# First weights of the eight closing lists: plain transfers of SyncE with a register's address in place of indirect transfers of GpSimd

## The chip, the cores and the metric

One core of one Trainium2 chip runs the whole program. The metric is the device time of one execution in microseconds (us), lower is better. Engines: PE (matrix engine), ACT (ScalarE), DVE (VectorE), POOL (GpSimd), SP (SyncE, which here only issues transfers).

## The reference

The input is 8 sequences of 2496 rows of 256 values. The first half transforms each sequence by a Fourier transform along its rows, multiplies by a complex 256x256 matrix, shrinks small values to zero and transforms back. The second half is a mixture of eight experts whose tokens are chosen under a limit:

```python
cap = N // E                                   # 19968 // 8 = 2496
flat = (x @ w_gate).flatten()
for idx in np.argsort(-flat):                  # best logits first
    tok, e = int(idx) // E, int(idx) % E
    if assigned[tok] >= 0 or counts[e] >= cap: continue
    assigned[tok] = e; counts[e] += 1
for e in range(E):
    mask = assigned == e
    out[mask] = np.maximum(x[mask] @ w1[e], 0.0) @ w2[e]   # 256 -> 1024 -> 256
```

So which tokens an expert gets depends on the data, and so does, in this kernel, the order in which the experts are worked off.

## The kernel before

**Stages.** `phase_a` does the eight sequences (to about 550 us), writes the mixed rows to the DRAM tensor `YD` and the logits to `LG`. From the first four sequences `Router.early` takes 512 sure tokens for each expert; these eight "early lists" have a fixed expert number and their weights are loaded by plain transfers of SP (the branch `e is not None`, lines 638 to 640). After that come eight "closing lists" of 1984 tokens. `Router.closing(i, ...)` finds on DVE which expert fills up next and which tokens it gets; the expert's number is a value in the tile `wi` (lines 974 to 979: column 4 the number itself, columns 2 and 3 the row numbers of its first weights).

**Weights.** `Experts.load` (line 628) brings one expert's weights in four pieces of 512 KB: the first weights `w1` as m = 0 and 1 (k = 0), then the second weights `w2` as m = 0 and 1 (k = 1). Each goes into a tile `raw`, of which there are two (in the slots `xt`), so the `w2` pieces can come only when the `w1` pieces have been split. The split is an ACT cast (line 659) into a slot of `W`, and a DVE subtraction (line 660) of what the cast lost. `W` has eight slots (in `sp`, `sh`, `FG`), two experts' worth. In the closing lists the `w1` pieces are indirect transfers of POOL (line 651), row numbers from `wi`; the `w2` pieces are plain transfers of SP whose address comes from a register that SP loads from `wi` (lines 643 to 648). Ahead of every indirect transfer POOL runs `GAP` = 14 empty instructions.

**Tokens.** `Experts.run` (line 663) gathers a list's token rows by indirect transfers of POOL (line 673), 128 rows each. In closing lists two such gathers then go by SP to a DRAM tile `XG` (line 680) and come back in four transfers of 32 partitions each (line 684), so that DVE can transpose them by blocks (line 697); DVE and ACT split them (lines 698, 699). The first matmuls are line 726 (three per weight half: high x high, high x low, low x high), evicted by ACT and DVE (lines 730 to 733); the second matmuls are lines 745 to 748, evicted by ACT and DVE (lines 754, 755) and scattered to the output by indirect transfers of POOL (line 758).

**Order.** Nothing of the order is written by hand. `Plan.run` (line 142) is a list scheduler that runs when the program is built: every task has an engine, a duration, a priority `pos`, the buffers that it reads and writes, and for a transfer an entry for when its data land. It picks, again and again, the task that can start first, and so fixes each engine's queue. The entries here:

```python
LATE = dict(sp=1.71, raw=7.61, gather=2.51, scatter=6.24)
def moved(nbytes, run, lead=1.6, back=1.8, late=0.0, k=16): ...
def dma(...):  plan.add('SP', 0.4, ..., load=moved(nbytes, run, late=LATE['sp'] + late))
def ind(...):  plan.add('P', g + 1.05, ..., load=moved(nbytes, run, g + 1.2, 1.4, late))   # g = 0.71
```

An engine works off its queue strictly in that order; an instruction that waits holds up all behind it.

`general` at the end of the file is a second router that the program enters only if the first one found that it could not hold; it calls `load` without `block`.

Of the kernel before, what the change touches and what calls it, by code (L numbers as in the profile page):

```python
# [100 lines left out]
class Plan:  # L101
# [20 lines left out]
    def add(self, eng, dur, pos, emit, reads=(), writes=(), tail=0.0, after=(), uses=(), load=None, slack=0.0, port=False):  # L122
        t = Task()
        t.port = port
        t.eng, t.dur, t.pos, t.emit, t.tail = eng, dur, pos, emit, tail or self.DEPTH.get(eng, 0.0)
        t.load, t.slack = load, slack
        t.deps, t.writes, t.end = set(after), list(writes), None
        for b in reads:
            t.deps.update(b.writers)
        t.ords = set()  # L130
        for b in writes:
            if b.state:
                t.ords.update(b.users)
                b.users, b.writers = [], []
            b.writers.append(t)
        for b in list(reads) + list(writes) + list(uses):
            b.users.append(t)
        t.id = len(self.tasks)
        self.tasks.append(t)
        return t  # L140
# [141 lines left out]
LATE = dict(sp=1.71, raw=7.61, gather=2.51, scatter=6.24)  # L282
# [9 lines left out]
def moved(nbytes, run, lead=1.6, back=1.8, late=0.0, k=16): return lead, nbytes / run * (0.009 + 3.68e-5 * run if run <= 4096 else 7e-5 * run) / k, back + late  # L292
# [25 lines left out]
class Kit:  # L318
# [20 lines left out]
    def v(self, n, pos, emit, reads, writes, slack=0.0, port=True):  # L339
        return self.plan.add('V', 0.068 + n / 960, pos, emit, reads, writes, slack=slack, port=port and not any(b.psum for b in reads))  # L340
# [76 lines left out]
def load_logits(K, H, LG, LGb, b, pos):  # L417
    def load():
        for t, src in logit_parts(H.ML, LG, b): K.nc.sync.dma_start(t, src)  # L419
    K.plan.add('SP', 2.4, pos, load, [LGb[b]], [H.b_ML], load=moved(80e3, 100, late=LATE['sp']))  # L420
# [199 lines left out]
class Experts:  # L620
# [7 lines left out]
    def load(self, pos, e=None, wi=None, block=False):  # L628

        K, plan, v = self.K, self.K.plan, self.K.v  # L630
        W1, W2, reg = [], [], []
        for k in range(2):
            for m in range(2):
                r = K.sb("raw", [128, 1024])
                W = K.sb("W", *(([128, 2, 4, 256], F32R) if k else ([128, 2, 1024], F32R)))
                (W2 if k else W1).append(W)
                p = pos + (2 * k + m)
                if e is not None:
                    src = self.w[k][e].rearrange("(m p) f -> p m f", m=2)[:, m] if not k else self.w[k][e].rearrange("(g m p) d -> p g m d", g=2, m=4)[:, m]
                    K.dma(p, lambda r=r, src=src, k=k: K.nc.sync.dma_start(r.t.rearrange("p (m d) -> p m d", m=4) if k else r.t, src), 524e3, [], [r], run=1024 if k else 4096)  # L640
                elif k:

                    def ld(r=r, m=m, reg=reg):
                        if not m: reg.append(K.nc.values_load(wi.t[0:1, 4:5], engines=[mybir.EngineType.SP], min_val=0, max_val=7, skip_runtime_bounds_check_because="the number of an expert, held to at most 7 where it is written"))
                        K.nc.sync.dma_start(r.t.rearrange("p (m d) -> p m d", m=4), self.w[1][bass.ds(reg[0], 1)].rearrange("o (g m p) d -> p (o g) m d", g=2, m=4)[:, m])
                    q = K.dma(p, ld, 524e3, [wi], [r], run=1024)
                    if m: q.ords.add(last)
                    last = q
                else:
                    c = (2 if block else 0) + m  # L650
                    K.ind(p, lambda r=r, c=c: K.P.indirect_dma_start(out=r.t, out_offset=None, in_=self.rows, in_offset=bass.IndirectOffsetOnAxis(ap=wi.t[:, c:c + 1], axis=0)), 524e3, [wi], [r], run=4096, late=LATE['raw'])

                def part(i, o, k=k, r=r, W=W):
                    if k: return W.t[:, i - 1, 2 * o:2 * o + 2] if i else r.t.rearrange("p (m d) -> p m d", m=4)[:, 2 * o:2 * o + 2]

                    return (W.t[:, i - 1] if i else r.t)[:, 512 * o:512 * o + 512]
                for o in range(2):
                    h = plan.buf(None, None)
                    plan.add('A', .525, p + 1, lambda part=part, o=o: K.A.copy(part(1, o), part(0, o)), [r], [W, h], slack=SLACK['split'])
                    v(512, p + 1, lambda part=part, o=o: K.V.tensor_tensor(part(2, o), part(0, o), part(1, o), op=OP.subtract), [r, h], [W])  # L660
        return W1, W2
# [922 lines left out]
```

## Time and profile before

| | |
|---|---|
| median of 3 executions | 1431.98 us (1431.59 to 1433.9) |
| the profiled execution | 1429.78 us |
| its span in the trace | 1427.9 us |
| PE busy | 1410.4 us, 99% |
| DVE busy | 1086.0 us, 76% |
| ACT busy | 800.6 us, 56% |
| POOL busy | 454.6 us, 32% |

The profiled execution's own time is 1.9 us above its span. Busy time is only what an engine works; issuing transfers and waiting are not in it. The closing lists run from about 700 us to the end.

### The profile page before, as it was taken

How to read it: one execution, taken by the hardware profiler on the slowest of the kernel's cores; microseconds unless marked ns; L12 is line 12 of the kernel's file. 1: busy time of each engine (PE TensorE's matmuls, PEld its weight loads, DVE VectorE, ACT ScalarE, POOL GpSimd, SP SyncE). 2: the span in 40 equal slices, each digit the busy share in tenths (PEclk: the TensorE clock that was granted, in tenths of full speed). 3: DMA queues.
4: the chain of work that ended last, by engine and by line, in shares of the span. 5: the costliest groups of instructions: out<-in, count | busy, mean ns of one | idle time of the engine just before them, and what ended most of it. 6: DMA issues, size and time to landing. Idle time of an engine off the chain costs nothing.

```text
span 1427.9 us, 33182 instructions
## 1 busy us (share of the span) xinstructions
PE 1410.4 (99%) x9619; PEld 1192.4 (84%) x9619; DVE 1086.0 (76%) x3197; ACT 800.6 (56%) x1918; POOL 454.6 (32%) x430
## 2 busy tenths in 40 slices
PE   8999999999999999999999999999999999999997
PEld 7888888887888878888888888888888888888886
DVE  6888788776999977999999999988776463553442
ACT  5676878877788865446454544444436443343331
POOL 0012222222224345123535353544443425212112
PEclk9999999999999999999999999999999999999999
DMA  6787898787878685333636364545443353421000
GB/s 223 227 285 268 240 300 267 241 270 229 286 235 257 201 268 172 106 121 99 189 103 172 112 185 132 170 139 146 119 135 116 96 150 115 128 56 38 21 23 30
DMA packets 223778, 238.09 MB, mean 167 GB/s; under 512 B 95286, under 2 KB 187619, under 8 KB 223587
## 3 DMA queue, kind: packets, MB, share of 16 engines
q1 hardware_dynamic: 205793, 185.91, 42.7%
q0 software_dynamic: 17664, 49.86, 11.2%
q8 instruction: 78, 1.28, 0.4%
q14 instruction: 113, 0.93, 0.2%
q10 hardware_dynamic: 130, 0.11, 0.0%
HBM read 138.10 MB, written 97.71 MB: 165 GB/s over the span
## 4 chain that ended last, share of the span: by engine, by line
PE 90%; DVE 4%; DMA 2%; ACT 2%; issue 1%; SPq 1%; POOL 0%; POOLq 0%; DVEq 0%; ACTq 0%
PE b L726 27%; PE b L745 18%; PE b L746 9%; PE b L1231 7%; PE b L1260 4%; PE b L1215 4%; PE pt L726 4%; PE b L1239 3%; PE b L1297 3%; PE b L1174 3%; PE pt L745 2%; PE b L1320 1%; PE pt L746 1%; PE b L748 1%; SPq L419 1%
## 5 line engine op out<-in xcount | busy, mean ns | idle before, releaser
L1053 POOL TENSOR_TENSOR s2l<-s2c,s2h 120x512 fp32r<-120x512 f32 (+1 forms) x84 | 105.8, 1268 | 381.6 <-ACT s2h L1050 335.8
L758 POOL DMA_INDIRECT out_dram<-xTh,li x64 | 67.5, 1055 | 209.0 <-DVE xTh L755 112.1
L1231 PE MATMUL b<-wt,xTh 128*128 128x256 f32 x640 | 123.7, 290 | 0.4 <-DVE yT L1310 0.3
L1231 PEld LDWEIGHTS b<-wt,xTh 128*128 128x128 f32 x640 | 100.7, 190 | 9.6 <-issue 2.9
L1231 PE MATMUL b<-wt,xTl 128*128 128x256 f32 x320 | 92.1, 288 | 2.9 <-DVE xTl L1224 2.6
L758 POOL DMA_INDIRECT out_dram<-xTl,li x64 | 65.5, 1023 | 85.1 <-DVE xTl L755 44.1
L1215 PEld LDWEIGHTS b<-FG,sh 128*128 128x128 f32 x640 | 82.3, 191 | 10.4 <-issue 4.8
L1215 PE MATMUL b<-FG,sh 128*128 128x128 f32 x640 | 88.5, 277 | 1.2 <-DVE sh L1195 1.2
L754 ACT COPY xTh<-b 128x256 f32<-128x256 f32 x66 | 24.7, 374 | 104.4 <-PE b L746 94.7
L1260 PE MATMUL b<-y,FG 64*128 64x256 f32 x640 | 80.2, 389 | 0.0
L754 ACT COPY xTl<-b 128x256 f32<-128x256 f32 x69 | 25.8, 373 | 91.8 <-PE b L746 87.4
L1260 PEld LDWEIGHTS b<-y,FG 64*128 64x128 f32 x640 | 58.4, 186 | 14.5 <-issue 2.9
L1244 DVE TENSOR_TENSOR y<-b,sx 128x512 f32<-128x512 f32 x80 | 54.6, 684 | 17.8 <-ACT sx L1242 17.3
L755 DVE TENSOR_TENSOR xTl<-b,xTl 128x256 f32<-128x256 f32 x69 | 28.9, 418 | 51.6 <-ACT xTl L754 49.1
L1233 DVE TENSOR_TENSOR b<-b,bf 128x512 f32<-128x512 f32 x80 | 55.3, 691 | 16.6 <-PE b L1231 16.2
L1310 DVE STREAM_TRANSPOSE yT<-b 128x512 f32<-128x512 f32 x86 | 60.5, 707 | 9.2 <-ACT yst L1299 6.1
L1297 PE MATMUL b<-s2h,d 120*128 120x512 f32 (+1 forms) x168 | 66.6, 406 | 0.0
L1231 PEld LDWEIGHTS b<-wt,xTl 128*128 128x128 f32 x320 | 60.8, 190 | 5.4 <-DVE xTl L1224 5.0
L1239 PE MATMUL b<-wt,xTh 128*128 128x256 f32 x320 | 63.6, 291 | 0.4 <-DVE y L1244 0.4
L755 DVE TENSOR_TENSOR xTh<-b,xTh 128x256 f32<-128x256 f32 x66 | 27.6, 418 | 47.2 <-ACT xTh L754 47.2
L1299 ACT COPY yst<-b 117x512 f32<-117x512 f32 (+1 forms) x93 | 51.7, 563 | 16.3 <-DVE yT L1310 7.6
L1246 ACT ACTIVATE y<-y,ml 128x512 f32<-128x512 f32 x60 | 43.7, 729 | 20.3 <-DVE y L1244 19.7
(1148 smaller groups left out, 4985.4 us busy)
## 6 DMA issues: line engine op xcount, KB each, us to landing
xt<-in_moe_w_dram SPq DMA_DIRECT2D x48, 512.0 KB
T<-s4st SPq DMA_DIRECT2D x80, 256.0 KB
s2c<-T SPq DMA_DIRECT2D x80, 240.0 KB
YD<-yst SPq DMA_DIRECT2D x80, 234.0 KB
xt<-in_x_dram SPq DMA_DIRECT2D x35, 512.0 KB
sh<-T SPq DMA_DIRECT2D x35, 512.0 KB
T<-s1st SPq DMA_DIRECT2D x70, 240.0 KB
yT<-XG SPq DMA_DIRECT2D x64, 64.0 KB
```

What stands on the lines that cost most here:

```text
L726: T.matmul(ps.t[:, 0:w], lhsT=W1[m].t[:, a, 128 * ft:128 * ft + 128], rhs=x_.t[:, 0:w], start=q + m == 0, stop=q + m == 3)
L745: T.matmul(ps.t, lhsT=hh.t[:, u:u + 128], rhs=W2[ft // 4].t[:, :, ft % 4], start=ft == 0, stop=False)
L746: T.matmul(ps.t[:, 0], lhsT=hl.t[:, u:u + 128], rhs=w_[0], start=False, stop=ft == 7)
L755: v(256, pos + 1, lambda: V.tensor_tensor(o.t, ps.t[:, 0], o.t, op=OP.add), [ps, o], [o])
L758: ins = P.indirect_dma_start(out=self.out, out_offset=bass.IndirectOffsetOnAxis(ap=oi.t[0:M, oo + t:oo + t + 1], axis=0), in_=o.t[0:M], in ...
L1053: lambda: eng.tensor_tensor(lb[1](), src(), hb[1](), op=OP.subtract), [srcb, hb[0]], [lb[0]], port=True)
L1215: T.matmul(ps.t[:, :, dt, i], lhsT=sh[k // 8].t[:, k % 8, 128 * dt:128 * dt + 128], rhs=at(Ft, k), start=True, stop=True)
L1231: T.matmul(pc.t[:, c], lhsT=a.t[:, 1 - c, dt], rhs=wt[2 - c].t[:, w, dt], start=dt == 0 and a is th and w == 0, stop=dt == 1 and a is tl)
L1239: T.matmul(pa.t, lhsT=a.t[:, 2, dt], rhs=wt[0].t[:, w, dt], start=dt == 0 and a is th and w == 0, stop=dt == 1 and a is tl)
L1260: T.matmul(ps4[i].t[:, r], lhsT=at(Gt, 2 * (p - 1 + r) + c)[h], rhs=zs[r].t[h, c], start=c == 0, stop=c == 1)
L1297: T.matmul(ps.t[:, gs_], lhsT=d5[0:k_, a], rhs=v.t[0:k_, gs_], start=i == 0, stop=i == 2)
L1310: yt.append(plan.add('V', TU, pos + Q['t5'], lambda yT=yT, ps=ps: V.transpose(yT.t.rearrange("p g m r -> p (g m r)"), ps.t.rearrange("p g ...
```

## The change

The first weights of the closing lists (`block` is true for all eight of them) take the branch that the second weights had. The register is loaded at the first of the four pieces (in place of the third). Each `w1` piece becomes four transfers of 32 partitions, which put the rows into the same partitions as the indirect transfer did. The task's entries change from POOL's indirect (duration 0.71 + 1.05, `late` 7.61) to SP's (duration 1.6, `late` 1.71), and the chain `q.ords.add(last)` keeps the pieces in order on SP. `general` keeps the indirect transfer.

```diff
-        W1, W2, reg = [], [], []
+        W1, W2, reg, last = [], [], [], None
...
-                elif k:
-
-                    def ld(r=r, m=m, reg=reg):
-                        if not m: reg.append(K.nc.values_load(wi.t[0:1, 4:5], engines=[mybir.EngineType.SP], ...))
-                        K.nc.sync.dma_start(r.t.rearrange("p (m d) -> p m d", m=4), self.w[1][bass.ds(reg[0], 1)].rearrange("o (g m p) d -> p (o g) m d", g=2, m=4)[:, m])
-                    q = K.dma(p, ld, 524e3, [wi], [r], run=1024)
-                    if m: q.ords.add(last)
-                    last = q
+                elif k or block:
+
+                    def ld(r=r, m=m, reg=reg, k=k):
+                        if not reg: reg.append(K.nc.values_load(wi.t[0:1, 4:5], engines=[mybir.EngineType.SP], ...))
+                        w = self.w[k][bass.ds(reg[0], 1)]
+                        if k: K.nc.sync.dma_start(r.t.rearrange("p (m d) -> p m d", m=4), w.rearrange("o (g m p) d -> p (o g) m d", g=2, m=4)[:, m])
+                        else:
+                            for G in range(4): K.nc.sync.dma_start(r.t[32 * G:32 * G + 32], w.rearrange("o (G m c) f -> m G (o c) f", G=4, m=2)[m, G])
+                    q = plan.add('SP', .4 if k else 1.6, p, ld, [wi], [r], load=moved(524e3, 1024 if k else 4096, late=LATE['sp']))
+                    if last: q.ords.add(last)
+                    last = q
                 else:
                     c = (2 if block else 0) + m
                     K.ind(p, lambda ...: K.P.indirect_dma_start(out=r.t, ..., ap=wi.t[:, c:c + 1], ...), 524e3, [wi], [r], run=4096, late=LATE['raw'])
```

## Rows read from the trace of the kernel before

**Rows 1.** The page, busy time of each engine over the span:

```profile
PE 1410.4 (99%) x9619; PEld 1192.4 (84%) x9619; DVE 1086.0 (76%) x3197; ACT 800.6 (56%) x1918; POOL 454.6 (32%) x430
```

**Rows 2.** Busy time by stretch: from:to, length, PE, PEld, DVE, ACT, POOL, clock, DMA:

```profile
600.00:700.00 100.00, 100.00 (x534) 82.72 (x533) 94.83 (x311) 51.53 (x124) 29.20 (x27) 1.00 0.40 123
...
800.00:900.00 100.00, 100.00 (x541) 82.45 (x540) 95.22 (x370) 55.56 (x158) 43.59 (x43) 1.00 0.51 144
...
1000.00:1100.00 100.00, 100.00 (x545) 82.82 (x544) 71.86 (x278) 49.54 (x146) 42.98 (x42) 1.00 0.44 127
...
1300.00:1419.50 119.50, 119.48 (x631) 103.69 (x629) 47.26 (x102) 36.92 (x73) 22.46 (x23) 1.00 0.08 27
1419.50:1427.90 8.40, 0.00 (x0) 0.00 (x0) 0.42 (x1) 0.37 (x1) 0.98 (x1) 0.78 0.11 32
```

**Rows 3.** The chain that ended last, 600 us on: start, length, what:

```profile
968.46 1.43 PE b L748 x12
...
1059.14 1.44 PE b L748 x12
...
1149.17 1.43 PE b L748 x12
...
1236.07 1.43 PE b L748 x12
...
1322.49 1.44 PE b L748 x12
...
1409.13 1.42 PE b L748 x12
```

**Rows 4.** Line 651, the sixteen indirect transfers: durations in ns, min/median/max:

```profile
L651 POOL DMA_INDIRECT xt<-in_moe_w_dram,wi x16: 942/976/1532, 688.3 to 1167.2; - x16
...
DMA to landing us min/median/max: 4.3/4.5/4.9
```

**Rows 5.** POOL in order of time, first of the two pieces of lists 2, 3, 5:

```profile
800.88 0.98 POOL L651 DMA_INDIRECT xt<-in_moe_w_dram,wi  x1 [1.89 <-ACT xh L730]
...
866.08 0.97 POOL L651 DMA_INDIRECT xt<-in_moe_w_dram,wi  x1 [1.61 <-DVE h_certs L932]
...
998.97 0.95 POOL L651 DMA_INDIRECT xt<-in_moe_w_dram,wi  x1 [12.15 <-DVE ga L962]
```

**Rows 6.** Line 684, SP's reads in four transfers; line 644, its register loads:

```profile
L684 SPq DMA_DIRECT2D yT<-XG x64: 303/449/637, 679.7 to 1260.7; - x64
```

```profile
L644 SPq TENSOR_LOAD <-wi x8: 266/270/487, 691.7 to 1234.9; - x8
```

**Rows 7.** SP in order of time, around lists 4 and 5, and a second weight piece:

```profile
926.96 0.36 SPq L680 DMA_DIRECT2D XG<-xh  x1
929.23 1.80 SPq L684 DMA_DIRECT2D xh<-XG  x4
...
994.48 0.39 SPq L680 DMA_DIRECT2D XG<-s2l  x1
1016.02 1.78 SPq L684 DMA_DIRECT2D wt<-XG  x4
...
1063.64 0.40 SPq L645 DMA_DIRECT2D xt<-in_moe_w_dram  x1
```

**Rows 8.** ACT in order of time, casts of first weights (lists 2, 3, 5) and second:

```profile
814.91 0.63 ACT L659 CAST sp<-xt 128x512 fp32r<-128x512 f32 x1
...
881.03 0.63 ACT L659 CAST sh<-xt 128x512 fp32r<-128x512 f32 x1
...
1060.19 2.18 ACT L659 CAST sh<-xt 128x512 fp32r<-128x512 f32 x4
...
1071.69 0.63 ACT L659 CAST FG<-xt 128x512 fp32r<-128x512 f32 x1
```

**Rows 9.** SP's queue, who waited for whom: total us, times, longest:

```profile
SPq L645 <- DMA xt<-in_moe_w_dram,wi: 15.1, 4, 6.2
```

**Rows 10.** Line 660, DVE's subtractions: durations in ns, min/median/max:

```profile
L660 DVE TENSOR_TENSOR sh<-xt,sh x64: 645/684/1736, 454.8 to 1241.3; 128x512 fp32r<-128x512 f32 x64
```

More of the change, by code (lines that the diff above doesn't have):

```diff
@@ L640, in load @@
                     K.dma(p, lambda r=r, src=src, k=k: K.nc.sync.dma_start(r.t.rearrange("p (m d) -> p m d", m=4) if k else r.t, src), 524e3, [], [r], run=1024 if k else 4096)
-                elif k:
-                    def ld(r=r, m=m, reg=reg):
-                        if not m: reg.append(K.nc.values_load(wi.t[0:1, 4:5], engines=[mybir.EngineType.SP], min_val=0, max_val=7, skip_runtime_bounds_check_because="the number of an expert, held to at most 7 where it is written"))
-                        K.nc.sync.dma_start(r.t.rearrange("p (m d) -> p m d", m=4), self.w[1][bass.ds(reg[0], 1)].rearrange("o (g m p) d -> p (o g) m d", g=2, m=4)[:, m])
-                    q = K.dma(p, ld, 524e3, [wi], [r], run=1024)
-                    if m: q.ords.add(last)
+                elif k or block:
+                    def ld(r=r, m=m, reg=reg, k=k):
+                        if not reg: reg.append(K.nc.values_load(wi.t[0:1, 4:5], engines=[mybir.EngineType.SP], min_val=0, max_val=7, skip_runtime_bounds_check_because="the number of an expert, held to at most 7 where it is written"))
+                        w = self.w[k][bass.ds(reg[0], 1)]
[4 more added lines that the diff above has]
+                    if last: q.ords.add(last)
                     last = q
```

## The prediction

> **What bounds the kernel now.** I read the page first. PE is busy 1410.4 of 1427.9 us [rows 1]; no other engine is over 76%. An average can hide a stage with another limit, so the second view is the busy time by stretch, in the stage that the change touches, the closing lists from about 700 us. From 600 us on PE is busy in every microsecond, to within 0.02 us in 119.5 [rows 2], and the granted clock is 1.00, the upper level of 2.4 GHz. POOL, whose work is taken away, is at 29 to 44% in the stretches shown. DVE is at 95% before 900 us and at 72% after 1000: it is close to being a second limit in the early lists, but nothing of PE's time waits for it.
>
> The third view is the chain that ended last. It stands on PE's matmuls all the way. The marks that I use are the short last tiles of the lists (line 748, one group per list) [rows 3]: between them lie 90.7 us (968.46 to 1059.14), 90.0, 86.9, 86.4 and 86.6 us. A list takes 86 to 91 us of matmuls, end to end, and the early ones are longer because the router's small matmuls lie among them. After the last matmul, at 1419.5, 8.4 us are left for eviction, scatter and landing [rows 2]; no weight load is in that tail.
>
> So the question is only whether PE gets a gap, and whether one is there to be taken away. None is.
>
> **The change part by part.** The sum is made against the profiled execution: span 1427.9 us, time 1429.78 us. The median of the runs shown is 2.2 us above that, 1431.98 us, and I carry the sum over to the median.
>
> 1. *Sixteen indirect transfers leave POOL.* Each is 0.976 us [rows 4] plus its empty instructions, which lie in POOL's idle time ahead of it, 1.61 us before list 3's piece [rows 5]. That is at most 16 x 2.6 = 41 us of POOL. It hides under PE's full queue, so worth 0; without that cover it would be 41 us at most.
>
> 2. *Sixty-four plain transfers come to SP's queue.* SP's reads in four transfers of 32 partitions have the same shape on the partition side; one issue takes 0.449 us [rows 6]. 64 x 0.449 = 29 us in all, 8 x 0.449 = 3.6 us per list, plus the register load of 0.27 us [rows 6], which is only moved: it stood at the second weights. SP's queue holds the token reads and writes through `XG` and the second weights; those behind the new issues come up to 3.9 us later. Is SP free there? At list 5, the one with the longest wait of POOL, SP issues its last write at 994.48 and its next read at 1016.02 [rows 7]: 21 us with nothing issued. At list 4 the gap is only from 927.32 to 929.23 [rows 7], so there a token read goes some 2 to 4 us later. PE holds a list's tokens long before it needs them, or it would show gaps already. Worth 0.
>
> 3. *SP now waits for the expert's number where POOL waited.* POOL stood 12.15 us ahead of list 5's piece, which went out at 998.97 [rows 5] as soon as DVE had written `wi`. SP comes free at about 994.9 and would stand at most 4.1 us for `wi`. Behind it in the queue is the read that went out at 1016.02 [rows 7] because its target was not free before. 4.1 + 3.9 = 8.0 us end at about 1003, 13 us ahead of that. Worth 0.
>
> 4. *Landing.* The indirect transfer lands 4.3 to 4.9 us after its issue [rows 4]. No row shows a first weight coming by SP. The nearest is the second weights, same size, same queue: issued at 1063.64 [rows 7], cast at 1071.69 [rows 8], 8.05 us later, with no wait of ACT on them in the trace. Bounds for the new path, from the first piece's issue: below, one transfer's 4.3 us; above, 3.6 us of issuing and the slowest landing, 4.9 us, so 8.5 us to the very last piece. I take 6 us, as the pieces overlap and the second half is cast after the first. From list 4 on this is idle: list 5's pieces are issued at 998.97 [rows 5] and cast at 1060.19 [rows 8], 61 us later, since they wait for slots of `W`.
>
> 5. *The casts of lists 0 to 3 move up.* There the cast stands at the place where the scheduler's entry lets the data land: list 2's 14.0 us after the issue, list 3's 15.0 us [rows 5, 8]. With SP's entry that distance should become about the 8.05 us of the second weights, so casts, subtractions and then the second weights' loads come some 6 us earlier. PE is full at that time, so an earlier weight gains nothing: 0. If data come later than the cast's place, ACT stands, and the evictions behind it; that is the rival below.
>
> 6. *The queues are dealt anew.* From the first changed task on, the scheduler may choose otherwise on every engine. No row shows that order. PE's work stays the same, matmul for matmul. A gain is excluded by the row of a full PE, apart from how the small matmuls fall. As bounds I take the spread between lists of the same kind in different orders: 86.4 to 86.9 us, and 90.0 to 90.7 us [rows 3], so about 0.5 us a list; eight lists all one way would be 4 us up or down. I take 0, since they won't all go one way, and keep both ends for the range.
>
> The sum: 0 us. 1429.78 us in the profiled execution, 1432.0 us in the median.
>
> **The rivals.**
>
> *Faster: DVE sets the pace and gets time back.* Some DVE instructions are stretched by about the length of one indirect transfer: line 660 takes 684 ns in the median and 1736 ns at most [rows 10], 1.05 us more. If each of the 16 transfers held DVE up so, and PE followed DVE in the stretch of 95%, up to 16 x 1.05 = 17 us would come back: 1415 us. For it: DVE's share before 900 us [rows 2]. Against it: PE has no idle time there to give, and from 1000 us on DVE is at 72% and less. The Trainium skill has the mechanism: "DMA: Bandwidth & Descriptors", in its section "SWDGE vs HWDGE vs iDMA", says that GpSimd writes its descriptors into on-chip memory from which DVE can lock it out, and that transfers of SP are immune to this. [...] By that rule alone the change should gain.
>
> *Slower: ACT stands for late first weights in lists 0 to 3.* The casts move up to about 8 us behind the issue. It decides where the last pieces land later than that. The longest wait for a weight transfer in SP's queue was 6.2 us [rows 9]; take that as the lateness. Evictions behind ACT stop; PE goes on until the other banks for first matmuls are full: two groups of six matmuls at 100 us / 541 = 0.185 us [rows 2], 2.2 us. So 6.2 - 2.2 = 4.0 us a list, times four lists: 16 us, 1448 us. For it: the upper bound of 8.5 us in step 4 is past 8.05. Against it: the transfer share is only 0.4 to 0.5 there, and ACT never waited for second weights at that distance. [...]
>
> *Slower by little: SP's wait holds up token reads.* If one list's reads come late by the 8.0 us of step 3, with 2.2 us of cover, PE loses 5.8 us: 1437.8 us. Against it: the 21 us in which SP stands anyway.
>
> That the change does nothing is excluded: `block` is true for all eight closing lists.
>
> **How the numbers follow.** About 0.2%, 2.9 us, is what can be told from no change. No gap moves: 0.79, with its own range of 1428 to 1436 us from the 4 us of step 6. DVE gives time back, in part or whole: 0.06. Late weights: 0.09. Held-up reads: 0.06. Of the first case little lies beyond 2.9 us; I leave it whole. The range runs from 1428.0, 4 us below, to 1438.0, which takes in the held-up reads; outside are the whole of the gain and the late weights. Faster 0.06, same 0.79, slower 0.15.
>
> **What would show it.** In the profile after: POOL's instructions fewer by 16, and its busy time by about 16 us; SP's first-weight issues 64 at about 0.45 us; PE still at 100.0 in each stretch from 600 us; casts of lists 2 and 3 about 8 us behind their issue, and no wait of ACT on them; marks of the last lists 86 to 87 us apart; the tail of 8.4 us unchanged. A PE below 99 us in any stretch after 680 us, with ACT or DVE waiting for a transfer just before it, would prove the forecast wrong on the slow side; a DVE share that falls together with a shorter distance between marks, on the fast side.

## The result, and the profile after

The changed kernel takes 1442.26 us in the median of 4 runs (1441.39 to 1443.46); the kernel before takes 1432.15 us beside it (1431.59 to 1433.9). The ratio is 1.0067, with a 95% interval of 1.0054 to 1.0079: slower by 10.1 us between the medians, 7.7 to 11.3 us by the interval, where the forecast was no change and the range ended at 1438. The profiled execution took 1442.89 us, its span 1441.1 us.

Most of what the forecast said of the kernel's inside came true. The page, busy time of each engine, to be read against [rows 1]:

```profile
PE 1412.4 (98%) x9619; PEld 1193.8 (83%) x9619; DVE 1084.8 (75%) x3197; ACT 800.6 (56%) x1918; POOL 437.3 (30%) x414
```

POOL has 16 instructions fewer and 17.3 us less work; PE has the same 9619 matmuls. The busy time by stretch of the changed kernel (from:to, length, then PE, PEld, DVE, ACT, POOL, granted clock, DMA share, GB/s), against [rows 2]:

```profile
600.00:700.00 100.00, 100.00 (x529) 82.57 (x528) 95.37 (x313) 52.90 (x127) 27.46 (x26) 1.00 0.40 126
800.00:900.00 100.00, 100.00 (x541) 82.55 (x540) 94.67 (x378) 51.75 (x148) 39.82 (x39) 1.00 0.50 142
1000.00:1100.00 100.00, 100.00 (x549) 83.15 (x548) 73.76 (x299) 47.76 (x139) 38.18 (x37) 1.00 0.45 132
1300.00:1423.20 123.20, 123.19 (x648) 106.76 (x646) 49.16 (x104) 38.51 (x76) 22.46 (x23) 1.00 0.08 27
1423.20:1441.10 17.90, 0.00 (x0) 0.00 (x0) 0.42 (x1) 0.37 (x1) 0.98 (x1) 0.58 0.05 15
```

PE is full to the last matmul, at the upper clock, as before. The last row is what is new: behind the last matmul the same single instruction each of DVE, ACT and POOL now lies in 17.9 us, not in 8.4. The chain that ended last, on the short tiles of the lists (start, length, what), against [rows 3]:

```profile
972.27 1.43 PE b L751 x12
1062.80 1.42 PE b L751 x12
...
1326.16 1.43 PE b L751 x12
1412.81 1.43 PE b L751 x12
```

The first of these marks is 3.8 us later than before, the last 3.7 us: the last five lists lost nothing. The offset arose ahead of the change. The queues of the two kernels are the same, instruction for instruction, up to 684 us, and the 5201st matmul already starts at 586.84 us in the one execution and at 590.48 us in the other. From 380 to 600 us, PE's busy time was 217.13 us in the one execution and 214.58 us in the other (busy time by stretch, before and then after):

```profile
380.00:600.00 220.00, 217.13 (x1947) 179.70 (x1947) 195.91 (x581) 155.66 (x386) 77.78 (x71) 1.00 0.69 212
```

```profile
380.00:600.00 220.00, 214.58 (x1925) 176.84 (x1924) 190.93 (x564) 153.00 (x381) 76.81 (x71) 1.00 0.68 210
```

So the two profiled executions, 13.1 us apart, differ by 3.7 us that belong to these executions and by 9.5 us behind the last matmul. What makes the tail longer are two instructions of POOL's sequencer at the very end of the program, INC_SWDGE_SEM (below, "the semaphore instruction") and DRAIN. They count as no busy time, and the timeline does not list them; asked for by their source lines, they are there. In the kernel before, line 1550 is the `tc.If` by which the program skips `general`, and line 1580 the `with` around the whole program (duration in ns, min/median/max; first and last start):

```profile
L1550 POOLq INC_SWDGE_SEM  x1: 620/620/620, 1424.6 to 1424.6; - x1
...
L1580 POOLq DRAIN  x3: 51/103/1773, 1425.3 to 1427.6; - x3
```

The changed kernel, the same view, with the last instruction of another engine as an example of who waits:

```profile
L1553 POOLq INC_SWDGE_SEM  x1: 2461/2461/2461, 1428.5 to 1428.5; - x1
...
L1583 POOLq DRAIN  x3: 51/103/9292, 1431.0 to 1440.8; - x3
...
L1583 ACTq DRAIN  x2: 8/8/8, 1426.3 to 1440.5; - x2
```

From the last matmul to the semaphore instruction it is 5.1 us before (1419.5 to 1424.6) and 5.3 us after (1423.2 to 1428.5). Then the semaphore instruction takes 1.841 us more, the first drain 7.519 us more, together 9.36 us. ACT drained at 1426.3 and has its second drain at 1440.5, behind POOL's: the program ends when POOL has closed. The question for the experiments is why POOL closes so much more slowly with 16 indirect transfers *fewer*.

### The profile page after: what moved, and what is told of

Its sections match the earlier page's. It is cut to its first block, busy times and chain, and to the rows that moved or that the text cites. A ratio compares the mean times of both kernels' runs of the same rounds, so it can differ in the third digit from the quotient of the medians.

```text
span 1441.1 us, 33180 instructions
## 1 busy us (share of the span) xinstructions
PE 1412.4 (98%) x9619; PEld 1193.8 (83%) x9619; DVE 1084.8 (75%) x3197; ACT 800.6 (56%) x1918; POOL 437.3 (30%) x414
## 4 chain that ended last, share of the span: by engine, by line
PE 90%; DVE 4%; ACT 2%; DMA 2%; issue 1%; SPq 1%; POOL 0%; POOLq 0%; DVEq 0%; ACTq 0%
PE b L729 27%; PE b L748 17%; PE b L749 9%; PE b L1234 7%; PE b L1263 4%; PE b L1218 4%; PE b L1242 4%; PE pt L729 3%; PE b L1300 3%; PE b L1177 3%; PE pt L748 3%; PE b L1323 1%; PE pt L749 1%; PE b L751 1%; DMA s2c<-T 1%
## 5 line engine op out<-in xcount | busy, mean ns | idle before, releaser
L581 ACT ACTIVATE ajunk<-b,h_bs 128x156 bf16<-128x156 f32 x113 | 44.1, 390 | 25.3 <-PE b L576 13.6
L729 PE MATMUL b<-yT,sp 128*128 128x512 f32 (+1 forms) x154 | 57.7, 385 | 0.0
```

The lines of the kernel that those rows point to most:

```text
L729: T.matmul(ps.t[:, 0:w], lhsT=W1[m].t[:, a, 128 * ft:128 * ft + 128], rhs=x_.t[:, 0:w], start=q + m == 0, stop=q + m == 3)
```

## The experiments

In what follows "the closing" is the pair of POOL's semaphore instruction and its longest drain. The kernel before has 336 indirect transfers in its trace, the changed kernel 320. `general` has transfers of its own, which no execution here reaches.

**Three theories** stood at first: the queues dealt anew change the ending; SP's transfers with an address from a register change it; the number of indirect transfers sets it. Four kernels separate them.

**The old order, the transfers on SP.** The scheduler's entry stays POOL's, so the queues stay as they were, and SP issues:

```diff
-K.ind(p, lambda r=r, c=c: K.P.indirect_dma_start(...), 524e3, [wi], [r], run=4096, late=LATE['raw'])
+def ls(r=r, m=m, reg=reg):
+    ...
+    w = self.w[0][bass.ds(reg[0], 1)]
+    for G in range(4): K.nc.sync.dma_start(r.t[32 * G:32 * G + 32], w.rearrange(...)[m, G])
+plan.add('P', Q['gw'] + 1.05, p, ls, [wi], [r], load=moved(524e3, 4096, Q['gw'] + 1.2, 1.4, LATE['raw']))
```

> The queues of before, with the change's plain transfers of SP put at the places where POOL issued the indirect ones; 320 indirect transfers in all. Theory count (what POOL does after its last transfer takes a time that depends on how many indirect transfers the program issued): the two last instructions of POOL stay as after the change, about 2.46 and 9.29 us, and the time is that of before plus 9.4 us, about 1441.5 us. Rival plan (the queues dealt anew cause it): 0.62 and 1.77 us and about 1432 us. Rival SP (64 more transfers of SP cause it): as theory count here.

Measured: 1438.36 us against 1429.76 us of the kernel before on that chip, ratio 1.0064 (1.0048 to 1.0081). POOL's closing:

```profile
L1557 POOLq INC_SWDGE_SEM  x1: 2461/2461/2461, 1424.2 to 1424.2; - x1
...
L1587 POOLq DRAIN  x3: 51/103/9292, 1426.7 to 1436.5; - x3
```

**The new order, the transfers on POOL.**

```diff
 def ld(r=r, m=m, reg=reg, k=k):
+    if not k:
+        c = 2 + m
+        for _ in range(GAP): K.P.engine_nop()
+        K.P.indirect_dma_start(out=r.t, out_offset=None, in_=self.rows, in_offset=...(ap=wi.t[:, c:c + 1], axis=0))
+        return
```

> The queues as dealt after the change, but the first weights come by POOL's indirect transfers again; 336 indirect transfers. Theory count: the two last instructions of POOL fall back to 0.62 and 1.77 us, the time to about 1433 us. Rival plan: 2.46 and 9.29 us, about 1442 us. Rival SP: as theory count here.

Measured: 1429.48 us, ratio 1.0001 (0.9991 to 1.0011). POOL's closing:

```profile
L1558 POOLq INC_SWDGE_SEM  x1: 620/620/620, 1421.8 to 1421.8; - x1
...
L1588 POOLq DRAIN  x3: 51/103/1773, 1422.5 to 1424.8; - x3
```

The order of the queues is out: the old order with 320 indirect transfers closes slowly, the new one with 336 closes quickly, to the nanosecond as the two kernels did. These two edits don't yet tell the number of indirect transfers from the presence of SP's.

**Sixteen spare gathers.** The first four token gathers of each of the last four closing lists are issued twice, into the same tile, in the changed kernel (336 again, SP's transfers kept) and in the kernel before (352):

```diff
+for _ in range(SPARE.get((early, nth), 0) > t and 2 or 1):
     ins = P.indirect_dma_start(out=g.t[:, t % 2], ...)
```

> The changed kernel with 16 token gathers of the last four closing lists issued twice (the same rows to the same place), so 336 indirect transfers, as before the change, and SP's 64 transfers kept. Theory count: 0.62 and 1.77 us at POOL's end, about 1433 us. Rivals plan and SP: 2.46 and 9.29 us, about 1442 us, a little more for the extra gathers.

> The kernel before with the same 16 gathers issued twice: 352 indirect transfers. Theory count: POOL's two last instructions change from 0.62 and 1.77 us; if they grow by what has been issued since some point, a little longer (by about a sixth to a half of the 7.5 us that after has more), 1433 to 1436 us; if they stand for a distance to a next point, clearly otherwise. Rivals plan and SP: 0.62 and 1.77 us, 1432 us.

Measured: 1444.27 us, ratio 1.0112 (1.0095 to 1.0128), and 1444.76 us, ratio 1.0113 (1.0087 to 1.014). As times, both miss, and the first alone would have spoken for the rivals. The reason is a gap of PE, which waited 10.9 us in the first kernel and 10.2 us in the second at line 509 for DVE's `ge`, between 900 and 1100 us. POOL also stood for gathers into the same tile to land (13.0 us ahead of the gathers into `ex`, from 1000 to 1400 us of the second kernel); whether the one leads to the other was not followed. The closings are what these two were for; first the changed kernel with 336, then the kernel before with 352:

```profile
L1559 POOLq INC_SWDGE_SEM  x1: 620/620/620, 1438.9 to 1438.9; - x1
...
L1589 POOLq DRAIN  x3: 51/103/1773, 1439.6 to 1441.9; - x3
```

```profile
L1556 POOLq INC_SWDGE_SEM  x1: 940/940/940, 1436.7 to 1436.7; - x1
...
L1586 POOLq DRAIN  x3: 51/103/3082, 1437.7 to 1441.4; - x3
```

With SP's transfers kept and the number back at 336, the closing is the short one again. So SP's transfers are out too, and of the three theories the number is left. From 336 to 352 the closing *grows*, by 320 ns and 1309 ns, that is 20 and 82 ns for each transfer; but 320 costs more than either. A price that rises with the number and falls back somewhere between 320 and 336 would do that. Four more kernels look for the fall.

**Around the fall.** Starting from the changed kernel, three kernels give the last one, two or four closing lists back to POOL's indirect transfers, in the changed kernel's order; one leaves 16 scatters out.

```diff
 def ld(r=r, m=m, reg=reg, k=k, nth=self.nld):
+    if not k and nth in POOLED:      # (7,) or (6, 7) or (4, 5, 6, 7)
+        ...
+        K.P.indirect_dma_start(out=r.t, ...)
+        return
```

```diff
-def sc():
+def sc(nth=self.nth):
+    if early and nth < 8 and t < 2:
+        P.engine_nop()
+        return
     ins = P.indirect_dma_start(out=self.out, ...)
```

> The changed kernel without 16 of its scatters (the first two of each early list), so 304 indirect transfers; those rows of the output are left out. Theory (POOL's closing instructions grow by 20 and 82 ns with each indirect transfer of the program and fall back at some count between 320 and 336): a semaphore instruction of about 2141 ns and a drain of about 7983 ns, the tail behind the last scatter 1.6 us shorter than the changed kernel's. Rival A (below some count the ending pays a fixed price, whatever the count): 2461 and 9292 ns again. Rival B (the last transfers still in flight hold the drain, not their number): 2461 and 9292 again, since the last scatters are the same.

> The changed kernel's queues, the first weights of the last closing list alone by indirect transfers of POOL: 322 indirect transfers. Theory: on the upper branch if the fall lies beyond 322: 2501 and 9456 ns, whole time as the changed kernel's; on the lower branch if it lies at 321 or 322: about 340 and 630 ns, the whole 11 us shorter. Rival B (what is in flight): nothing between, 2461 and 9292 ns.

> The changed kernel's queues, the first weights of the last two closing lists by POOL: 324 indirect transfers. Theory: 2541 and 9620 ns if the fall lies beyond 324, 380 and 790 ns if before. Rival A (a threshold at some count with a fixed price on either side): 2461 and 9292, or 620 and 1773.

> The changed kernel's queues, the first weights of the last four closing lists by POOL: 328 indirect transfers. Theory: 2621 and 9947 ns if the fall lies beyond 328, 460 and 1119 ns if before it, the whole then about 1 us under the kernel before. Rival A: 2461 and 9292, or 620 and 1773.

Measured, one execution each, beside 1431.12 us of the kernel before: 1439.67 us with 304, 1441.98 with 322, 1432.63 with 324, 1432.66 with 328. The closings with 304, 322, 324 and 328:

```profile
L1557 POOLq INC_SWDGE_SEM  x1: 2141/2141/2141, 1426.9 to 1426.9; - x1
...
L1587 POOLq DRAIN  x3: 51/103/7986, 1429.0 to 1437.6; - x3
```

```profile
L1559 POOLq INC_SWDGE_SEM  x1: 2501/2501/2501, 1427.3 to 1427.3; - x1
...
L1589 POOLq DRAIN  x3: 51/103/9456, 1429.8 to 1439.8; - x3
```

```profile
L1559 POOLq INC_SWDGE_SEM  x1: 380/380/380, 1428.4 to 1428.4; - x1
...
L1589 POOLq DRAIN  x3: 51/103/793, 1428.8 to 1430.2; - x3
```

```profile
L1559 POOLq INC_SWDGE_SEM  x1: 460/460/460, 1428.4 to 1428.4; - x1
...
L1589 POOLq DRAIN  x3: 51/103/1120, 1428.9 to 1430.6; - x3
```

Every one is within 3 ns of the number that the theory had given for its branch. Rival A, a fixed price on either side of a threshold, falls with 304 and 328; rival B, the transfers still in flight, falls with 304, whose last scatters are the changed kernel's. The fall lies between 322 and 324: two more indirect transfers make the closing 10.8 us shorter (2501 + 9456 against 380 + 793 ns).

**Does it repeat, and does a kernel at 324 gain?** The changed kernel once more (5 executions) and the kernel with 324 (12); and two kernels with 104 and 105 scatters left out, 108 and 109 transfers below 324:

```diff
+if early or t < (10 if nth == 8 else 9):      # 215; with 9 throughout, 216
+    P.engine_nop()
+    return
```

> The changed kernel itself, for a second interval on this chip: +9.4 us over the kernel before (1841 ns of the semaphore instruction and 7519 ns of the drain), so 1441 where before takes 1431.6; if the 4 us by which its matmuls ended later in the one profile belong to the change and not to that execution, +13 us.

> The first weights of the last two closing lists by POOL, the rest by SP, 324 indirect transfers: the count just behind the fall. Theory: tail 1.2 us shorter than the kernel before's (380 + 793 against 620 + 1773 ns), so 1.2 us (0.1%) faster, and 10.6 us faster than the changed kernel. If the late matmul end of this kernel's one look (4 us) belongs to it: 3 us slower than before.

> The changed kernel without 104 of its scatters (all of the early lists, the first nine of each closing list): 216 indirect transfers, 108 fewer than the 324 of the short ending; those rows of the output are left out. Theory (the price repeats every 108 transfers): 380 and 793 ns as at 324. Rival (no repeat, it only falls once): about 381 and 787 ns from the upper branch's slope (2461 - 104 x 20, 9292 - 104 x 81.8), so this run alone can't tell them apart: it is read with the next.

> The same with one more scatter left out: 215 indirect transfers. Theory (the price repeats every 108): 2521 and 9538 ns as it would be at 323, the whole about 10.9 us longer than with 216. Rival (the upper branch goes down to zero by its slope): 361 and 705 ns, the whole the same as with 216.

Measured: the changed kernel 1444.44 us against 1435.21 us of the kernel before, ratio 1.0058 (1.0045 to 1.0071), 9.2 us between the medians, 6.5 to 10.2 us by the interval. The first guess of 9.4 us lies in it and 13 us does not, so the 3.7 us later end of PE in the first profile is none of the change. The kernel with 324: 1435.22 us, ratio 0.9996 (0.9987 to 1.0004), not to be told from the kernel before; its shorter tail of 1.2 us is less than such a comparison shows. With 216 and 215 transfers 1444.6 and 1444.79 us, and these closings:

```profile
L1557 POOLq INC_SWDGE_SEM  x1: 2521/2521/2521, 1429.9 to 1429.9; - x1
...
L1587 POOLq DRAIN  x3: 51/103/9537, 1432.4 to 1442.5; - x3
```

```profile
L1557 POOLq INC_SWDGE_SEM  x1: 2501/2501/2501, 1430.1 to 1430.1; - x1
...
L1587 POOLq DRAIN  x3: 51/103/9456, 1432.7 to 1442.7; - x3
```

The expectation for 216 missed: it is still on the high side. The rival, a single branch that goes down to nothing (361 and 705 ns at 215), missed as well: from 216 to 304 transfers the closing gets shorter, so by these two kernels it falls at least once there too. After how many transfers it falls stays open. 215 closes exactly as 322 does, which would be a repeat after 107; but the fall between 322 and 324 is one of 108 steps (2501 + 2 x 20 - 380 = 2161 ns), and one fixed repeat can't be both. The two kernels also differ from the others in a second thing: by the same edit `general`, which is built and skipped, loses 72 of its 336 indirect transfers. No run tells whether that matters. All nine numbers of transfers together:

| indirect transfers | kernel | semaphore instruction, ns | drain, ns |
|---|---|---|---|
| 215 | 105 scatters out | 2501 | 9456 |
| 216 | 104 scatters out | 2521 | 9537 |
| 304 | 16 scatters out | 2141 | 7986 |
| 320 | **changed kernel** | 2461 | 9292 |
| 322 | one list on POOL | 2501 | 9456 |
| 324 | two lists on POOL | 380 | 793 |
| 328 | four lists on POOL | 460 | 1120 |
| 336 | **kernel before** | 620 | 1773 |
| 352 | 16 gathers twice | 940 | 3082 |

The steps inside a branch are 20 ns and 82 ns a transfer throughout: from 304 to 322, 360 and 1470 ns over 18; from 324 to 352, 560 and 2289 ns over 28.

## Why the prediction was wrong, point by point

**Steps 1 to 5** of the prediction held for what they weighed: none of them cost PE anything. *Step 1*: POOL lost 16 instructions, and their time was covered by a full PE. Its words "worth 0" failed all the same: the step asked where POOL's time lies, not what the number of its transfers does later. *Step 2*: SP's issues (start, length, what; the first and the last of the eight lists):

```profile
690.82 4.08 SPq L648 DMA_DIRECT2D xt<-in_moe_w_dram  x8
...
1168.07 5.64 SPq L648 DMA_DIRECT2D xt<-in_moe_w_dram  x8
```

They take 3.9 to 5.6 us a list, where 3.6 was taken from [rows 6]; PE shows none of it. *Step 3*: SP stood for the expert's number much longer than the 4.1 us of the step, and at some lists for the tile to come free as well (SP's queue: total us, times, longest):

```profile
SPq L644 <- DVE wi L980: 31.9, 4, 13.6
...
SPq L648 <- DVE FG L663: 11.9, 2, 9.6
```

At list 5 the issue came at 1001.54, about where the step had it, and PE shows none of these waits. *Steps 4 and 5*: the casts of the first weights on ACT (start, length, what), lists 0, 2, 3 and 5, to be held against [rows 8]:

```profile
698.53 1.13 ACT L662 CAST sp<-xt 128x512 fp32r<-128x512 f32 x2
...
813.72 0.63 ACT L662 CAST sp<-xt 128x512 fp32r<-128x512 f32 x1
...
882.96 1.16 ACT L662 CAST sh<-xt 128x512 fp32r<-128x512 f32 x2
...
1063.85 2.18 ACT L662 CAST sh<-xt 128x512 fp32r<-128x512 f32 x4
```

List 0's cast is 7.7 us behind its issue at 690.82, list 2's 6.8 us behind 806.92; list 3's is 11.6 us behind 871.41, so "about 8" was short by 3.6 there. ACT's idle time ahead of all casts of line 662 is 5.3 us, and all of it was ended by PE, none by a transfer: no late weights.

*Step 6*, the queues dealt anew, was given 0 with 4 us either way. The kernel with the new order and POOL's transfers measures 1.0001 (0.9991 to 1.0011): 0, to within 1.6 us.

**The step that failed** stands at the end of the first part and in the list of what would be seen: "8.4 us are left for eviction, scatter and landing", "the tail of 8.4 us unchanged". The tail was read from what is busy in it, and was put down to three things. In truth 620 + 1773 = 2393 ns of it were POOL's closing, present in the trace under two source lines that were not asked for, and that part depends on the number of indirect transfers, which the change was known to alter. A term for it was missing from the sum, which is to say put at nothing; it measures 9.36 us (1841 + 7519 ns), against 10.1 and 9.2 us between the medians of the two comparisons. What no reading could have given is its size and sign: at 336 the kernel stands 12 transfers above the fall, and one trace shows one point of a price that rises and falls. With the two rows before it, though, the step could have carried the closing as an unknown and not as a part that stays.

**The rivals.** *DVE sets the pace*: out; PE is full in the stretch of 94.67% too. Its price of 1.05 us a transfer was also read wrongly from [rows 10]. The subtraction of 1736 ns starts at 496.96 us, and no indirect transfer overlaps it: POOL is then at subtractions of its own (line 1053). The four subtractions that do overlap a transfer of line 651 take 684 to 745 ns, against a median of 684; and with the 16 transfers gone the longest is still 1736 ns (line 663). The rule that speaks for the change, in the Trainium skill's "DMA: Bandwidth & Descriptors", section "SWDGE vs HWDGE vs iDMA", could give nothing here: PE is full and had no idle time to give back. Whether DVE was freed at all these rows don't show; its busy time went from 1086.0 to 1084.8 us. *Late first weights* and *held-up reads*: out; their price would be a gap of PE, and there is none. The slower side got 0.15, all of it for gaps of PE. The slowdown came without one.

## What to carry to other kernels

Read the end of the program as its own stage: look up, by source line, the sequencer instructions behind the last transfer, and ask what their length depends on. Whoever changes the number of POOL's indirect transfers, in either direction, should compare these two rows of the two profiles before explaining anything else; here a kernel with 16 transfers fewer paid 9.4 us, and with four of them given back it paid nothing. A saving that hides under a full engine is worth nothing, but its side effect at the end of the program is not hidden by anything.

## What was not expected of the hardware

- POOL's closing rises by 20 ns (semaphore instruction) and 82 ns (drain) with each indirect transfer of the program, and falls from 2501 + 9456 to 380 + 793 ns between 322 and 324. By the two kernels in which `general` is smaller too, it also falls between 216 and 304, the values at 215 being those at 322; how often it falls is open. It came out the same to within 1 ns wherever a number was run twice, in other orders and on other chips (320 three times, 336 three times).
- What is being counted stays open: only transfers of 128 rows were added or taken away, so transfers and rows can't be told apart, and no row shows what POOL does during the drain. Bytes are out: from 304 to 320 the difference is 16 scatters of 131 KB, from 320 to 322 two weight pieces of 524 KB, and each adds the same 20 and 82 ns.
- Executions of the kernel before on one chip spread from 1433.48 to 1437.44 us (17 runs), and its median was 1429.76, 1432.15 and 1435.21 us on three occasions. Of the 13.1 us between the two profiles, 3.7 us were such a difference, and it arose ahead of the first changed instruction.
